# Where v's first copies and the tail groups' turns are issued in the opening of a segment-recurrent attention kernel

## The chip, the cores and the metric

The kernel runs on one core of one Trainium2 chip. The metric is the device time of one execution in microseconds; lower is better. Several executions of each kernel are timed, and their median counts.

## The reference, cut to what matters

A pre-norm block: attention over segments of 32 tokens, in which 8 memory rows are carried from each segment to the next, and then a dense part with a squared ReLU. x is 2048 x 640 in bf16, 32 heads of 128; Wq, Wk and Wv are 640 x 4096, Wo is 4096 x 640.

```python
for s in range(n_seg):                       # 64 segments, in order
    xs = x[:, s*32:(s+1)*32]                 # layernormed
    h = concatenate([mem, xs], axis=1)       # 8 memory rows + 32 tokens
    q, k, v = h @ Wq, h @ Wk, h @ Wv         # per head
    p = softmax(where(mask, q @ k.T * Dh**-0.5, -1e9))
    o = (p @ v) @ Wo
    mem = o[:, :8]                           # the next segment needs this
    outs.append(o[:, 8:])
h = x + concatenate(outs)
h2 = h + (relu(layernorm(h) @ w1 + b1) ** 2) @ w2 + b2
```

## The kernel before

**Rows.** A segment's 40 rows are split. Its 8 memory rows and its first 24 tokens make the 32 main rows, which must wait for the segment before. Its last 8 tokens, the tail, depend on no memory. Four segments make a block; the tails of a block's four segments are 32 rows, and those of four blocks, 128 rows, are a tail group: ("t", 0) to ("t", 3). For a tail group, `load_tail_rows` loads the rows, `ln_stats` takes the statistics (two on VectorE, their aggregation there, and two small steps on GpSimd for the inverse root, L174 and L175), `ln_norm` writes the normalized rows `xn` on VectorE (L188), and `ln_transpose` turns them on TensorE (`pt`, L118) and lets ScalarE copy the result to `hTt` (L218). There is one buffer for `xn`.

**Order.** Each engine executes its instructions in the order in which the program writes them; no scheduler moves them. Waits between engines and the DMA queues go over semaphores. SyncE issues nearly all loads and stores, and one that must wait holds back all issued behind it.

**The opening.** `start()` (L788) computes the first segment's q, k and v and, beside that, the q, k or v rows of tails. It has three streams, each over the five chunks of 128 rows of one weight as they arrive: `stream("v")`, `stream("q")`, `stream("k")`. For a chunk, a stream multiplies the main rows (two banks `pa`, n = 0 and 1) and block 0's tail rows (two more banks of `pa`), and then runs up to `k` closures from the list `units`. The four banks of `pa` are one PSUM buffer, so a stream cannot begin before the one ahead of it has been copied out. After the last chunk of v, VectorE copies the two main banks to `v` (L814) and ScalarE the two tail banks to `row` tiles (L263 by way of `tail_out`), with a DMA to the scratch tensor `vt_d` behind each (L360, on ScalarE's queue for block 0). After q and k, ScalarE copies all four banks, VectorE transposes each copy into `qT` or `kT` (`flip`), and GpSimd moves the tail parts.

`units` holds matmuls that fill TensorE while the weights arrive: `tail_units(b, "v")` are ten closures of four matmuls, two accumulations of five, for block b's tails; each accumulation ends in `tail_out`, a copy by ScalarE. Those v tails of later blocks are kept in places that are free in the beginning (`parked`: five slices of `hnT0`, then `ht0`, `oTts` and others), and are stored to `vt_d` later. `row` tiles come from `rowtile()`, four buffers in turn, and a tile is free again when its transpose or its store is done. `ps` tiles come from `mm` (three banks), `pc` from the bank that later holds `sm` and `pw`.

On SyncE's queue, in the order of issue: x rows, Wv, the second tail group's rows, Wq, the third group's rows (`load_tail_rows(2)`), Wk, Wo in eight pieces (`load_wo`), the next block's x rows, then block 0's tails of v read back from `vt_d` in part (`tails_v_in`; the first part on ScalarE's queue, L414), and the fourth group's rows from within step 0.

**Steps.** `step(b, sp)` then takes one segment: projections of q, k, v where `start` has not done it, scores, softmax (`soft1`, `soft2`), values, the 16 output rounds over Wo (`wo_rounds`, accumulating in `pw`), the token rows' softmax (`tokens_sum`), and `mem_to_hT`, in which VectorE and ScalarE turn the 8 new memory rows into the next step's input (L294 to L297). `run(fill, n)` puts further tail matmuls between these; `late`, `mid`, `owed`, `soon` and `stores` are other lists of closures that a step runs at fixed places. For step 0, the one with `ready`, three places of `run(fill, n)` take 2, 3 and 3 closures, and the rest follows behind output round 12.

Of the kernel before, what the change touches and what calls it, by code (L numbers as in the profile page):

```python
# [16 lines left out]
def kernel(  # L17
# [238 lines left out]
    def rowtile():  # L256
        return s2.tile([128, 512], BF16, tag="row", name="row", bufs=4)
# [38 lines left out]
        for a in range(2):  # L296
            nc.vector.tensor_tensor(out=hT4[64 * a:64 * a + 64, :, sp, 0:M], in0=tr[0:64, a, :, 0:M], in1=tc_[:, a], op=ALU.add)  # L297

    fill, late, mid, owed = [], [], [], [[], [], []]

    def run(q, n):
        while n > 0 and q:
# [21 lines left out]
    def tail_quarters(b, which, n, u):  # L324
        if which == "v":
            wr = wv[:].rearrange("p (c k n u f) -> p c n k u f", c=DC, k=G, n=2, u=2)
            cols = lambda c, k: wr[:, c, n, k, u]
        else:
            w = {"q": wq, "k": wk}[which]
            wr = w[:].rearrange("p (c g j n k e) -> p c n k g j e", c=DC, g=G, n=2, j=4, k=4)  # L330
            cols = lambda c, k: wr[:, c, n, k, 2 * u:2 * u + 2]
        st = {}

        def unit(cs):
            def f():
                if 0 in cs:
                    st["ps"] = mmtile()
                for c in cs:
                    for k in range(4):
                        matmul(st["ps"][32 * k:32 * k + 32, 0:256], lhsT=tail_rows(b, c), rhs=cols(c, k),  # L340
                               start=(c == 0), stop=(c == DC - 1))
                if DC - 1 in cs:
                    row = rowtile()
                    evac_row(which, row[:, 0:256], st["ps"][:, 0:256])
                    if which == "v":
                        nc.sync.dma_start(out=vt_d[b, 2 * n + u], in_=row[:, 0:256])
                        return
                    dst = tails[b][which]
                    late.append(lambda: nc.vector.transpose(out=dst[:, n * 16 + u * 8:n * 16 + u * 8 + 8, 0:32],
                                                            in_=row[:, 0:256].rearrange("p (h e) -> p h e", e=32)))  # L350
            return f
        return [unit(cs) for cs in ((0, 1), (2, 3), (4,))]

    def tail_out(b, which, n, ps):
        kept = which == "v" and 0 < b and len(parked) > 0
        row = parked.pop(0)() if kept else rowtile()[:]
        evac_row(which, row, ps)
        if which == "v":
            def store(eng=nc.sync):
                eng.dma_start(out=vt_d[b, 2 * n:2 * n + 2].rearrange("j r f -> r j f"),  # L360
                              in_=row.rearrange("r (j f) -> r j f", j=2))
            if kept:
                stores.append(store)
            else:
                store(nc.sync if b else nc.scalar)
            return
        if n == 0:
            tails.setdefault(b, {})[which] = s2.tile([128, H, 32], BF16, tag=which + "Tt", name=which + "Tt")
        dst = tails[b][which]
        late.append(lambda: flip(row, dst, n))  # L370
# [86 lines left out]
    def step(b, sp, v=None):  # L457
# [123 lines left out]
        token_scores(0)  # L581
        if ready:
            load_tail_rows(3)
            run(fill, 2)
        if not ready:
            proj(wv, "half", lhs, 0, ps0, 2, DC)
            nc.scalar.copy(out=v[:, 0:512], in_=ps0[:])
# [8 lines left out]
        if not last:  # L596
            soft1(1)
        if ready:
            run(fill, 3)
        po = pop.tile([128, G, 512], F32, tag="po", name="po")  # L600
        if not ready:
            proj(wv, "half", lhs, 1, ps1, 2, 3)
# [33 lines left out]
        wo_rounds(main, pw, 6, 8)  # L636
        if ready:
            tokens_sum()
        run(fill, 3 if ready else 1)
        wo_rounds(main, pw, 8, 12)  # L640
        if ready:
            run(fill, len(fill) - 6)
# [145 lines left out]
    def start():  # L788
# [11 lines left out]
        def stream(which, w, dst, k=0):  # L800
            pa = pop.tile([128, 4, 512], F32, tag="po", name="pa")
            for c in range(DC):
# [6 lines left out]
                if c < DC - 1:  # L809
                    run(units, k)  # L810
                    run(late, 100)
            for n in range(2):
                if which == "v":
                    nc.vector.tensor_copy(out=v[:, n * 512:(n + 1) * 512], in_=pa[:, n, :])  # L814
                else:
                    row = rowtile()[:]
                    evac_row(which, row, pa[:, n, :])
# [5 lines left out]
                for n in range(2):  # L823
                    tail_out(0, which, n, pa[:, 2 + n, :])

        ln_stats(("t", 1))
        ln_norm(("t", 1))
        ahead = [tail_units(1, "v"), tail_units(2, "v", (mmtile, lambda: chn.tile([128, 512], F32, tag="ch", name="pc")))]
        units += [a[n * DC + c] for c in range(DC) for a in ahead for n in range(2)]
        stream("v", wv, None, 4)  # L830
        units += tail_units(3, "v")
        units.append(lambda: ln_transpose(("t", 1))())
        units += tail_units(4, "v") + tail_units(5, "v") + tail_units(6, "v")
        run(units, 10)
        load_tail_rows(2)
        load_w(wk, A_Wk)
        load_wo()
        load_x(1)
        stream("q", wq, qT, 7)
        ln_stats(("t", 2))  # L840
        ln_norm(("t", 2))
        for n in range(2):
            spread(n)
        units += tail_units(7, "v")
        units.insert(9, lambda: ln_transpose(("t", 2))())
        units += tail_units(1, "q") + tail_units(8, "v")
        run(units, 14)
        tails_v_in(0, nc.scalar, 0, 1)
        tails_v_in(0, nc.sync, 1, 4)
        stream("k", wk, kT, DC)  # L850
        units += tail_units(1, "k")
        run(units, 100)
        return v
# [19 lines left out]
    for b in range(NB):  # L873
        for sp in range(4):
# [3 lines left out]
            if b == 0:  # L878
# [12 lines left out]
                    mid.append(lambda: ln_norm(1))  # L891
                if sp == 3:
                    ln_turn(1)
            elif b < NB - 1:
                if sp == 0:
                    fill += tail_units(b + 1, "q")[0:DC] + tail_quarters(b + 1, "q", 1, 0)
# [148 lines left out]
```

## Time and profile before

| | us |
|---|---|
| median of three timed runs | 955.13 (953.6 to 955.96) |
| the profiled execution, its own time | 958.96 |
| span of its trace | 957.2 |
| TensorE busy in the span | 929.5 (97%) |
| VectorE busy | 702.1 (73%) |
| ScalarE busy | 546.6 (57%) |
| GpSimd busy | 257.3 (27%) |

Times count from the start of the span. In the profile PE is TensorE's matmuls, PEld its weight loads, DVE VectorE, ACT ScalarE, POOL GpSimd, SP SyncE; "SPq" and "ACTq" in a view of DMAs or of a timeline are the instructions with which these engines issue DMAs. A row of a timeline has the start, the time from the first to the last instruction of the group, engine, line, operation, the tile written and the tiles read, the count, and in brackets how long the engine idled before it and what ended that. L114 and L118 are the lines of the helpers for matmul and transpose, so matmuls are told apart by their tiles: `ps<-wv,hTt` is a v tail unit, `pa<-wq,hT` the stream of q, `pw<-wo,oT` an output round. PEclk is the clock that was granted to TensorE, 1.00 for full speed.

### The profile page before, as it was taken

The page shows a single profiled execution, that of the slowest core. Times are in us where ns is not written, and L with a number is a line of the kernel's source. Part 1 is how long each engine was busy: PE and PEld are TensorE (multiplying, and loading weights), DVE is VectorE, ACT ScalarE, POOL GpSimd, SP SyncE. Part 2 cuts the span into 40 slices and gives each one's busy share as a digit, 9 for nine tenths or more (in the row PEclk, how much of TensorE's full clock was granted, in tenths as well). Part 3 has the DMA queues.
Part 4 walks back from the last instruction along what each step waited for, and adds up shares of the span by engine and source line. Part 5 has one row for each costly group of instructions (what it writes and reads, how often), then busy time and mean ns, then how long its engine had stood idle before and what let it go on. Part 6 is the DMA issues. An engine that isn't in the chain of part 4 may idle for free.

```text
span 957.2 us, 57556 instructions
## 1 busy us (share of the span) xinstructions
PE 929.5 (97%) x25883; PEld 569.8 (60%) x25883; DVE 702.1 (73%) x2136; ACT 546.6 (57%) x1342; POOL 257.3 (27%) x798
## 2 busy tenths in 40 slices
PE   5799999999999999999999999999999998999998
PEld 2346566666566666665666666666666565555555
DVE  3157788888888888888888787878788888476532
ACT  2446666666666666666666666666666665523321
POOL 1012222222222222222222222222222233254300
PEclk9899999999999999999999999999999999999999
DMA  9963210101010101010101010101010110643320
GB/s 357 404 201 96 61 34 9 34 9 34 9 33 10 34 9 34 10 34 9 31 11 32 11 32 10 32 12 31 11 32 11 53 43 21 201 111 85 94 55 28
DMA packets 60710, 56.74 MB, mean 59 GB/s; under 512 B 27560, under 2 KB 56624, under 8 KB 58544
## 3 DMA queue, kind: packets, MB, share of 16 engines
q1 hardware_dynamic: 59776, 52.74, 18.4%
q8 instruction: 202, 3.31, 1.5%
q14 instruction: 44, 0.36, 0.1%
q10 hardware_dynamic: 688, 0.33, 0.1%
HBM read 38.37 MB, written 9.44 MB: 50 GB/s over the span
## 4 chain that ended last, share of the span: by engine, by line
PE 92%; DVE 3%; DMA 2%; ACT 1%; issue 1%; POOL 0%; ACTq 0%; DVEq 0%
PE ps L114 62%; PE pw L114 16%; PE y L114 6%; PE po L114 5%; DMA xt<-in_A_x_dram 2%; PE sm L114 1%; PE pa L114 1%; DVE lnst L170 0%; DVE wk L968 0%; DMA vt_d<-row 0%; ACT otc L295 0%; DVE kTt L266 0%; DVE qT L266 0%; DVE otr L294 0%; DVE kT L266 0%
## 5 line engine op out<-in xcount | busy, mean ns | idle before, releaser
L114 PEld LDWEIGHTS <-hT 128*32 128x32 bf16 x8358 | 219.4, 96 | 136.5 <-DVE hT L297 10.4
L114 PE MATMUL pw<-wo,oT 128*32 128x320 bf16 x4224 | 178.7, 301 | 0.2
L114 PE MATMUL ps<-wv,hT 128*32 128x512 bf16 x2520 | 177.8, 380 | 0.2 <-ACT row L483 0.2
L114 PE MATMUL ps<-wq,hT 128*32 128x512 bf16 (+1 forms) x3143 | 160.9, 337 | 4.6 <-DVE hT L297 4.5
L114 PE MATMUL ps<-wk,hT 128*32 128x512 bf16 (+1 forms) x2575 | 160.3, 374 | 0.0
L652 POOL TENSOR_TENSOR pkt<-ek,rk 128x64 bf16<-128x64 bf16 x64 | 19.2, 300 | 411.4 <-DVE rk L650 398.2
L114 PEld LDWEIGHTS <-oT 128*32 128x32 bf16 x4224 | 97.0, 96 | 54.2 <-DVE oT L252 19.5
L266 DVE STREAM_TRANSPOSE qT<-row 128x512 bf16<-128x512 bf16 x128 | 89.9, 703 | 27.7 <-ACT row L261 24.6
L261 ACT ACTIVATE row<-ps 128x512 bf16<-128x512 f32 (+1 forms) x170 | 94.1, 562 | 17.7 <-PE ps L114 11.9
L967 ACT ACTIVATE wv<-ps,b1f 128x512 bf16<-128x512 f32 (+1 forms) x56 | 37.5, 673 | 67.2 <-PE ps L114 66.3
L440 ACT CAST oT<-po 128x512 bf16<-128x512 f32 x128 | 74.6, 586 | 0.1
L114 PEld LDWEIGHTS <-hTt 128*32 128x32 bf16 x1660 | 45.0, 99 | 34.6 <-issue 5.7
L295 ACT COPY otc<-otr 64x40 f32<-64x40 f32 x126 | 28.0, 223 | 65.5 <-DVE otr L294 65.0
L451 POOL COPY qz<-qT 128x96 bf16<-128x96 bf16 x126 | 33.3, 265 | 115.0 <-DVE mx L502 57.8
L114 PEld LDWEIGHTS <-v 32*128 32x128 bf16 x4064 | 42.1, 91 | 33.0 <-issue 18.4
L263 ACT CAST row<-ps 128x512 bf16<-128x512 f32 (+1 forms) x113 | 61.1, 557 | 1.1 <-PE ps L114 0.4
L114 PE MATMUL y<-wq,wk 128*128 128x320 bf16 x448 | 61.1, 299 | 0.0
L626 DVE TENSOR_REDUCE zk<-ek 128x8 f32<-128x320 bf16 x64 | 31.1, 486 | 38.3 <-ACT ek L625 38.3
L483 ACT CAST row<-ps 128x256 bf16<-128x256 f32 x126 | 40.8, 375 | 31.4 <-PE ps L114 30.4
L608 ACT CAST v<-ps 128x512 bf16<-128x512 f32 x63 | 36.9, 586 | 29.8 <-PE ps L114 29.8
L266 DVE STREAM_TRANSPOSE kT<-row 128x512 bf16<-128x512 bf16 x65 | 45.7, 703 | 10.8 <-ACT row L263 7.5
L114 PEld LDWEIGHTS <-wk 128*128 128x128 bf16 x448 | 40.6, 98 | 19.9 <-issue 5.0
(112 smaller groups left out, 1625.2 us busy)
## 6 DMA issues: line engine op xcount, KB each, us to landing
wv<-in_A_Wv_dram SPq DMA_DIRECT2D x5, 1024.0 KB
wq<-in_A_Wq_dram SPq DMA_DIRECT2D x5, 1024.0 KB
wk<-in_A_Wk_dram SPq DMA_DIRECT2D x5, 1024.0 KB
vt<-vt_d SPq DMA_DIRECT2D x60, 64.0 KB
xt<-in_A_x_dram SPq DMA_DIRECT2D x18, 160.0 KB
wo<-in_A_Wo_dram SPq DMA_DIRECT2D x2, 1280.0 KB
wq<-in_B_w_dram SPq DMA_DIRECT2D x1, 2080.0 KB
o_all<-o SPq DMA_DIRECT2D x128, 15.0 KB
```

The source lines that it names most:

```text
L114: nc.tensor.matmul(*a, **k)
L261: nc.scalar.mul(out=row, in_=ps, mul=scale)
L263: nc.scalar.copy(out=row, in_=ps)
L266: nc.vector.transpose(out=dst[:, n * 16:(n + 1) * 16, 0:32], in_=row.rearrange("p (h e) -> p h e", e=32))
L295: nc.scalar.copy(out=tc_[:, a], in_=tr[64:128, a, :, 0:M])
L440: nc.scalar.copy(out=oTg[:, n, :, :, M:NK], in_=po[:, :, n * 128:(n + 1) * 128].rearrange("p g (j q) -> p g j q", q=32))
L451: nc.gpsimd.tensor_copy(out=d.rearrange("p a (j f) -> p a j f", j=3)[:, :, :, 0:M], in_=src[:, :, 0:3, :])
L483: nc.scalar.copy(out=row[:, u * 256:(u + 1) * 256], in_=ps[:, u * 256:(u + 1) * 256])
L608: nc.scalar.copy(out=v[:, 512:1024], in_=ps1[:])
L626: nc.vector.tensor_reduce(out=zk[:], in_=ek[:], op=ALU.add, axis=AX.X)
L652: nc.gpsimd.tensor_tensor(out=pkt[:], in0=ek[:, :, SEG:NK], in1=rk[:].unsqueeze(2).to_broadcast([128, HG, TL]), op=ALU.mult)
L967: nc.scalar.activation(out=r[:, 0:w], in_=ps[:, 0:w], func=ACT.Relu, bias=b1f[:, fc:fc + 1], scale=1.0)
```

## The change

- After the stream of v, ScalarE and no longer VectorE copies the two main banks; so ScalarE copies all four.
- `tail_out` lets VectorE copy the two v tail banks of block 2.
- The second tail group, ("t", 1): statistics and norm are written behind the stream of v, and no longer ahead of it; its turn comes behind eight of block 3's ten v tail units, and no longer behind all ten, and two empty closures stand a little behind it in the list; six closures and not ten are run ahead of the loads of Wk.
- The third tail group, ("t", 2): statistics and norm are written inside the stream of q, behind its second chunk's units, and no longer behind that stream; its turn is put at the end of the units that are left from the stream of q, ahead of block 7's, and no longer behind block 7's ninth.
- Fifteen closures and not fourteen are run between the streams of q and k; within the stream of k six per chunk and not five.
- In step 0 the three places take 4, 2 and 2 closures of `fill`, not 2, 3 and 3.
- From step 3 of block 0 on, two slices of `hnT0` serve as row tiles (`spare`), one each, for the next two tail banks or quarters that would take a buffer from `rowtile()`.

```diff
-    fill, late, mid, owed = [], [], [], [[], [], []]
+    fill, late, mid, owed, spare = [], [], [], [[], [], []], []
...
                 if DC - 1 in cs:
-                    row = rowtile()
+                    row = spare.pop(0) if spare else rowtile()
                     evac_row(which, row[:, 0:256], st["ps"][:, 0:256])
...
     def tail_out(b, which, n, ps):
         kept = which == "v" and 0 < b and len(parked) > 0
-        row = parked.pop(0)() if kept else rowtile()[:]
-        evac_row(which, row, ps)
+        row = parked.pop(0)() if kept else spare.pop(0) if spare else rowtile()[:]
+        if which == "v" and b == 2:
+            nc.vector.tensor_copy(out=row, in_=ps)
+        else:
+            evac_row(which, row, ps)
...
         if ready:
             load_tail_rows(3)
-            run(fill, 2)
+            run(fill, 4)
...
         if ready:
-            run(fill, 3)
+            run(fill, 2)
...
-        run(fill, 3 if ready else 1)
+        run(fill, 2 if ready else 1)
...
                     run(units, k)
                     run(late, 100)
+                if which == "q" and c == 1:
+                    ln_stats(("t", 2))
+                    ln_norm(("t", 2))
             for n in range(2):
                 if which == "v":
-                    nc.vector.tensor_copy(out=v[:, n * 512:(n + 1) * 512], in_=pa[:, n, :])
+                    nc.scalar.copy(out=v[:, n * 512:(n + 1) * 512], in_=pa[:, n, :])
...
-        ln_stats(("t", 1))
-        ln_norm(("t", 1))
         ahead = [tail_units(1, "v"), tail_units(2, "v", (mmtile, lambda: chn.tile([128, 512], F32, tag="ch", name="pc")))]
         units += [a[n * DC + c] for c in range(DC) for a in ahead for n in range(2)]
         stream("v", wv, None, 4)
+        ln_stats(("t", 1))
+        ln_norm(("t", 1))
         units += tail_units(3, "v")
-        units.append(lambda: ln_transpose(("t", 1))())
-        units += tail_units(4, "v") + tail_units(5, "v") + tail_units(6, "v")
-        run(units, 10)
+        units.insert(8, lambda: ln_transpose(("t", 1))())
+        units.insert(11, lambda: None)
+        units.insert(12, lambda: None)
+        for b in (4, 5, 6):
+            units += tail_units(b, "v")
+        run(units, 6)
         load_tail_rows(2)
...
         stream("q", wq, qT, 7)
-        ln_stats(("t", 2))
-        ln_norm(("t", 2))
         for n in range(2):
             spread(n)
-        units += tail_units(7, "v")
-        units.insert(9, lambda: ln_transpose(("t", 2))())
-        units += tail_units(1, "q") + tail_units(8, "v")
-        run(units, 14)
+        units.append(lambda: ln_transpose(("t", 2))())
+        units += tail_units(7, "v") + tail_units(1, "q") + tail_units(8, "v")
+        run(units, 15)
         tails_v_in(0, nc.scalar, 0, 1)
         tails_v_in(0, nc.sync, 1, 4)
-        stream("k", wk, kT, DC)
+        stream("k", wk, kT, 6)
...
                 if sp == 3:
                     ln_turn(1)
+                    spare += [hnT0[:, c, :] for c in range(2)]
```

From step 1 on, the instructions stand in the same order on every engine as before.

## The prediction

> **What bounds the kernel now.** I read the page first: it says that TensorE is busy nearly throughout, and its slices say where it isn't.
>
> ```profile
> span 957.2 us, 57556 instructions
> PE 929.5 (97%) x25883; PEld 569.8 (60%) x25883; DVE 702.1 (73%) x2136; ACT 546.6 (57%) x1342; POOL 257.3 (27%) x798
> PE   5799999999999999999999999999999998999998
> PEclk9899999999999999999999999999999999999999
> DMA  9963210101010101010101010101010110643320
> ```
>
> A slice is 24 us. Only the first two show a PE below 9, a granted clock below full, and DMA engines at 9. All that the change moves lies there and in step 3 of block 0. I therefore read the timeline of PE next, over the first 110 us, with what ended each idle stretch:
>
> ```profile
> 20.41 2.34 PE L114 MATMUL ps<-wv,hTt 128*32 128x512 bf16 x40
> 24.93 0.87 PE L114 MATMUL pa<-wq,hT 128*32 128x512 bf16 x8 [2.17 <-ACT row L263]
> ...
> 28.11 2.75 PE L114 MATMUL ps<-wv,hTt 128*32 128x512 bf16 x24 [0.81 <-ACT hTt L218]
> ...
> 45.16 0.45 PE L118 MATMUL pt<-ident,xn 128*128 128x128 bf16 x5 [3.75 <-DVE xn L188]
> ...
> 56.73 2.33 PE L114 MATMUL ps<-wk,hTt 128*32 128x512 bf16 x40
> ...
> 62.33 1.00 PE L114 MATMUL pw<-wo,oT 128*32 128x320 bf16 x24
> ...
> 64.42 1.26 PE L114 MATMUL pw<-wo,oT 128*32 128x320 bf16 x32
> ...
> 67.70 1.26 PE L114 MATMUL ps<-wq,hT 128*32 128x512 bf16 x20 [0.73 <-DVE hT L297]
> ```
>
> Three waits are the opening's own: 2.17 us before Wq's first chunk, 0.81 us for the turned second tail group, 3.75 us for the normalized third. 24 matmuls took 2.75 us at 28.11, 40 took 2.34 us at 20.41: the clock. The windows view, cut where the clock changed, shows it:
>
> ```profile
> 21.75:25.16 3.41, 1.24 (x25) 0.54 (x21) 1.40 (x3) 1.17 (x2) 0.00 (x0) 1.00 1.02 423
> 25.16:28.58 3.42, 2.61 (x29) 0.95 (x21) 0.00 (x0) 2.32 (x4) 0.00 (x0) 0.50 1.00 407
> 28.58:31.99 3.41, 3.41 (x40) 1.19 (x36) 0.00 (x0) 0.91 (x2) 0.00 (x0) 0.50 1.05 411
> 45.64:49.06 3.42, 3.42 (x36) 1.38 (x36) 0.00 (x0) 2.16 (x3) 0.00 (x0) 0.50 1.07 363
> ```
>
> (Length, busy time of PE, PEld, DVE, ACT, POOL, granted clock, DMA share, GB/s.) A window with PE busy 1.24 of 3.41 us was followed by half clock; one of 2.61 of 3.42 us did not end it; full ones did. The waits cost twice: 6.73 us idle, then 10.25 us at half clock.
>
> **The opening's compute path.** From 20.41 to the end of Wk's tail units (56.73 + 2.33 = 59.06) PE takes 38.65 us. Off go 6.73 us of idling and half of the 9.44 us of matmuls at half clock (10.25 less the 0.81 idle inside), 4.72 us: 27.2 us of matmuls at full clock remain, the same in number after the change. Now the edits. The chain of waits shows how the first wait came about:
>
> ```profile
> 20.90 0.58 POOL lnrs L175
> ...
> 21.50 0.45 DVE xn L188
> 21.95 1.21 DVE v L814 x2
> ...
> 23.24 0.59 ACT row L263
> ...
> 23.86 0.40 ACTq L360
> ```
>
> v's copies on DVE stand behind the second group's norm, which waits for its rows; ACT's two tail banks wait for v; PE's first Wq matmul waits for ACT. After the change ACT takes all four banks, from the end of stream v's last matmul, about 0.2 us after the next ones' start at 20.41. Its four q evictions show the pace:
>
> ```profile
> 39.52 2.06 ACT L261 ACTIVATE row<-pa 128x512 bf16<-128x512 f32 x4 [0.71 <-PE pa L114]
> ```
>
> So 2.06 us plus the store's issue between the last two (0.40 and some gaps, together 0.6): pa is free at 23.3 rather than 24.9. PE has then run 24 tail matmuls instead of 40, to 21.8, and idles 1.4-1.5 us. The two tail banks given to DVE take about 0.6 us each there, before the norm; xn comes at 23.3, and PE asks for it only after Wq's first chunk and two units (24.6): hidden by 1.3 us. The turned group then has two units and the next chunk's sixteen matmuls (some 1.3 us) over ACT's first copy; the 0.81 us goes, at most 0.1 stays.
>
> The third group is now normalized in stream q, on DVE ahead of q's flips. Its rows are issued right behind Wq:
>
> ```profile
> 6.46 12.54 SPq L132 DMA_DIRECT2D wq<-in_A_Wq_dram  x5
> 19.41 0.54 SPq L150 DMA_DIRECT2D ht<-in_A_x_dram  x1
> ```
>
>  At 420 GB/s that queue (Wv, Wq and the x tiles, 11 MB from 2 us on, with a slower first 6 us) is through at about 32.5; the norm (two statistics 0.87, their sum 0.2, POOL 0.23 and 0.58, xn 0.45, with gaps 2.5 us) ends at 35.0, and q's rows reach DVE only at 34. PE reaches the turn, 27.2 us of matmuls being spread as before, at 35.4. If rows and norm came 2 us later, PE waited 2 us of the 3.75; I take 0.2. POOL's two small rsqrt steps move ahead of qT's copies with it, and nobody waits for those before the scores. Six units per chunk and the inserted empty units change only the order of matmuls: nothing. Sum of the path: 27.2 + 1.45 + 0.3 = 28.95 us, to 49.4: 9.7 us earlier than 59.06.
>
> **What is late next.** That isn't the gain, since the same queue still has to bring Wo. The windows view again, its last columns above all:
>
> ```profile
> 59.50:60.00 0.50, 0.50 (x35) 0.17 (x18) 0.50 (x2) 0.49 (x1) 0.00 (x0) 1.00 0.98 266
> 60.00:60.50 0.50, 0.17 (x4) 0.00 (x0) 0.15 (x2) 0.32 (x2) 0.29 (x1) 1.00 0.14 49
> ```
>
> The engines are full to 60.0 and nearly idle at 60.0-60.5: Wo's last piece lands at about 60.2, whatever PE does, as the bytes ahead of it are the same. Wo is 5.2 MB (32 x 128 x 640 in bf16); at some 340 GB/s (363 at 45.64, 266 at the end) it fills 44.7 to 60.2, so Wk is in before the new path uses its last chunk (46.0). The first half of Wo is there at 52.4, when the new path wants it (62.33 - 9.7 = 52.6), but the second output rounds, at 64.42 before, would come at 54.7 and need the second half piece by piece; the last six matmuls start at 60.3. Before, the accumulation ended at 65.68 and the block turn began at 66.60 behind VectorE's softmax of the tokens:
>
> ```profile
> 66.19 0.48 DVE L626 TENSOR_REDUCE zk<-ek 128x8 f32<-128x320 bf16 x1 [0.54 <-ACT ek L625]
> 66.60 0.57 DVE L294 STREAM_TRANSPOSE otr<-pw 128x160 f32<-128x160 f32 x2
> ...
> 68.60 0.87 DVE L170 BATCH_NORM_STATS2 lnst<-ht 128x6 f32<-128x320 bf16 x2
> ```
>
> After, that softmax is done by 57; the turn starts at 60.7 and step 1, 1.10 us on (66.60 to 67.70), at 61.8: **5.9 us earlier**. The fourth group's statistics (68.60, so 62.7 now) need rows that SyncE loads behind Wo:
>
> ```profile
> 60.23 3.17 SPq L148 DMA_DIRECT2D ht<-in_A_x_dram  x4
> ```
>
> Four issues of 0.8 us, the last ones freed by Wo's last landings, would end near 61.7, and the rows be there 1 to 2 us on: VectorE, with q's flips queued behind its statistics, might stand for 0 to 0.8 us. I count 0, as the next term covers it.
>
> **The clock again.** From 54.9 to 60.3 PE has 26 short output matmuls, 0.9 us. A 3.41 us stretch of that is busier than 26% nowhere in the middle, below the 1.24 of 3.41 us that halved the clock above. So it halves between 58.4 and 61.8. One window at half clock loses 1.7 us, of which the wait for the turn hides up to 1.1; a second follows if the first is partly idle. Ends: 0.6 and 2.8 us; I take 1.6.
>
> **Rows that are spare.** In step 3 of block 0 ACT waited for a row buffer whose store was under way:
>
> ```profile
> 108.97 0.65 ACT L483 CAST row<-ps 128x256 bf16<-128x256 f32 x2 [0.91 <-DMA vt_d<-row]
> 108.03 0.27 PE L114 MATMUL sm<-kT,qz 128*32 128x40 bf16 x16
> 110.98 0.26 PE L114 MATMUL po<-pTm,v 32*128 32x8 bf16 x16 [0.18 <-DVE pTm L518]
> 120.52 0.27 PE L114 MATMUL sm<-kT,qz 128*32 128x40 bf16 x16
> 122.80 0.26 PE L114 MATMUL po<-pTm,v 32*128 32x8 bf16 x16
> ```
>
> Scores to values took 2.95 us there, 2.28 us a step later. Two spare rows give 0.6 us (0 to 0.67). Moving fill units within step 0 of the block only fills PE's gaps earlier; their number is the same.
>
> **Sum.** 5.9 - 1.6 + 0.6 = 4.9 us. The profiled execution took 958.96 us (span 957.2 and 1.76 around it), so 954.1 for its like; against the median of 955.13: **950.2 us**. Own ends: gate 2.8 and no spare gain, 952.1; gate 0.6, 949.2.
>
> **The rivals.** (a) The clock stays full, if the short output bursts keep it: no single gap there would be longer than about 1.6 us (5.4 us less 0.9 of work, in three or more waits). Row 21.75:25.16, half clock after a window with 2.17 us of idling in one piece, speaks against it. Gain 5.9 - 0.5 (VectorE then does wait for the fourth group) + 0.6 = 6.0: 949.1. Chance 0.15. The Trainium skill, TensorE: Matmul & The Clock Gate, section on HAM oscillation, is on this rival's side: it gives some 3.4 us of idling as what throttles, and the trace, with 2.17 us, does not agree. (b) The timed executions of before have a shorter opening than the profiled one, which is 3.8 us above their median. If fewer half-clock windows are the reason, up to 4.7 us of the opening are gone there already, while the new end is held at 60.2 by Wo; with half of it the gain is 2.5: 952.6, with all 0.2: 954.9. Against it: the 3.75 us wait alone empties most of a window wherever that falls. No change, chance 0.22. (c) Slower: SyncE's loads share semaphores with ACT's transfers.
>
> ```profile
> SPq L163 <- DMA vt<-vt_d: 7.5, 4, 5.7
> 47.43 3.16 ACTq L414 DMA_DIRECT2D vt<-vt_d  x4
> ```
>
> In the new order Wo's third load waits for ACT's first vt load, the fifth to seventh for the other three. ACT issues them after the third group's turn, by my path at 39-42, and they land 5.7 us later, by 48; two Wo loads queued ahead last to 52.4. Past that point every microsecond delays Wo by one; break-even is 4.9 us later, at 57, and a slip to 61 gives 959. It needs ACT some 13 us late: 0.07, with whatever else holds SyncE.
>
> **How the numbers follow.** Forecast 0.56, (a) 0.15, (b) 0.22, (c) 0.07. Differences below 0.3% (2.9 us) can't be told from none here: faster needs under 952.3, which the forecast's own range meets and (b) mostly does not. Faster 0.69, same 0.23, slower 0.08. The range leaves out (c), most of (b)'s upper half and the unlikeliest end of (a): 948.3 to 953.8; forecast and (a) alone, 948.3 to 952.1.
>
> **What would show it.** Right: PE's first Wq chunk at 23.3; no wait for DVE xn near 40; Wk's tail units over at about 49; a wait of `pw` on `wo`'s DMA near 55 to 60; a half-clock window after 58; step 1 at 62-63.5; no wait on vt_d<-row near 108. Wrong: Wo landing before 58 or after 62; pa waiting for ACT after 23.8; the third group's norm still ending a PE wait; steps 1 to 3 longer than before by more than the gate.

## The result: 2.5 us faster, about half of the forecast

The changed kernel took 952.86 us (median of 22 executions) against 955.4 (22): ratio 0.9975, interval 0.9965 to 0.9984. In two later comparisons it was 950.33 against 953.3 (0.9968, 0.9953 to 0.9982) and 951.02 against 953.09 (0.9978, 0.9963 to 0.9993). So 2 to 3 us are gained, where 4.9 were forecast; the first median, 952.86, lies inside the whole range on record and 0.8 us above the end of the forecast's own one (952.1). Its profiled execution took 952.75 (span 950.9), 6.2 less than the profiled one of before. The gap between 6.2 and 2.5 is what has to be explained.

PE's timeline of the changed kernel, the opening, with the rows that answer to those of before:

```profile
19.60 1.46 PE L114 MATMUL ps<-wv,hTt 128*32 128x512 bf16 x24
22.54 0.61 PE L114 MATMUL pa<-wq,hT 128*32 128x512 bf16 x8 [1.47 <-ACT row L263]
...
23.95 0.45 PE L118 MATMUL pt<-ident,xn 128*128 128x128 bf16 x5
24.33 0.61 PE L114 MATMUL ps<-wv,hTt 128*32 128x512 bf16 x8
...
35.72 0.45 PE L118 MATMUL pt<-ident,xn 128*128 128x128 bf16 x5
36.61 1.26 PE L114 MATMUL ps<-wv,hTt 128*32 128x512 bf16 x20 [0.44 <-ACT oTt L263]
...
47.40 2.34 PE L114 MATMUL ps<-wk,hTt 128*32 128x512 bf16 x40
...
56.78 0.72 PE L114 MATMUL pw<-wo,oT 128*32 128x320 bf16 x14 [1.48 <-DMA wo<-in_A_Wo_dram]
57.68 0.31 PE L114 MATMUL pw<-wo,oT 128*32 128x320 bf16 x2 [0.18 <-DMA wo<-in_A_Wo_dram]
58.54 0.45 PE L114 MATMUL pw<-wo,oT 128*32 128x320 bf16 x6 [0.55 <-DMA wo<-in_A_Wo_dram]
59.39 0.31 PE L114 MATMUL pw<-wo,oT 128*32 128x320 bf16 x2 [0.40 <-DMA wo<-in_A_Wo_dram]
60.33 0.53 PE L114 MATMUL pw<-wo,oT 128*32 128x320 bf16 x6 [0.62 <-DMA wo<-in_A_Wo_dram]
60.48 2.94 PE L114 MATMUL ps<-wv,hTt 128*32 128x512 bf16 x24
62.95 1.89 PE L114 MATMUL ps<-wq,hT 128*32 128x512 bf16 x20
```

The 2.17 us wait is 1.47, those of 0.81 and 3.75 are gone. Wk's tail units are over at 49.74 (59.06 before), and then PE waits five times for Wo; the last piece is in at 60.3, as before. Behind it 24 fill matmuls take 2.94 us: half clock. The windows view shows how little PE did before that (length, busy PE, PEld, DVE, ACT, POOL, granted clock, DMA share, GB/s):

```profile
19.61:23.02 3.41, 1.94 (x40) 0.88 (x36) 1.87 (x5) 2.24 (x5) 0.79 (x2) 1.00 1.02 423
53.73:57.15 3.42, 1.95 (x60) 1.10 (x55) 2.82 (x6) 0.73 (x2) 0.00 (x0) 1.00 1.07 362
57.15:60.56 3.41, 1.66 (x28) 0.54 (x23) 0.08 (x1) 0.00 (x0) 0.00 (x0) 1.00 0.77 258
60.56:63.97 3.41, 3.41 (x40) 2.76 (x35) 1.82 (x7) 1.97 (x5) 1.57 (x4) 0.50 0.22 73
```

For comparing kernels I take the turns: the end of VectorE's second L297 operation, which completes a step's input. VectorE's timeline has them; first the turns of steps 1, 2, 4 and 5 of the kernel before, then of the changed one:

```profile
67.22 0.42 DVE L297 TENSOR_TENSOR hT<-otr,otc 64x40 bf16<-64x40 f32 x2
79.01 0.43 DVE L297 TENSOR_TENSOR hT<-otr,otc 64x40 bf16<-64x40 f32 x2
...
103.16 0.42 DVE L297 TENSOR_TENSOR hT<-otr,otc 64x40 bf16<-64x40 f32 x2
115.65 0.43 DVE L297 TENSOR_TENSOR hT<-otr,otc 64x40 bf16<-64x40 f32 x2
```

```profile
61.53 0.43 DVE L297 TENSOR_TENSOR hT<-otr,otc 64x40 bf16<-64x40 f32 x2
74.83 0.42 DVE L297 TENSOR_TENSOR hT<-otr,otc 64x40 bf16<-64x40 f32 x2
...
98.69 0.42 DVE L297 TENSOR_TENSOR hT<-otr,otc 64x40 bf16<-64x40 f32 x2 [0.29 <-ACT otc L295]
110.56 0.42 DVE L297 TENSOR_TENSOR hT<-otr,otc 64x40 bf16<-64x40 f32 x2
```

The turn behind step 0 (that of step 1) is 5.69 us earlier. The next step gives 1.5 back, 13.29 us for 11.79: the half-clock window. Steps 2 and 3 bring 0.3, and from step 4 to step 5 come 0.6. At step 5 the changed kernel is 5.09 ahead (110.98 for 116.07), and it stays 4.5 to 5.8 ahead to the last turn. The three terms of the sum, 5.9, 1.6 and 0.6, are all there, between these two executions, as 5.7, 1.5 and 0.6.

### The profile page after: what moved, and what is told of

Same layout as the page of the kernel before. It is cut to its first block, busy times and chain, and to the rows that moved or that the text cites. A ratio compares the mean times of both kernels' runs of the same rounds, so it can differ in the third digit from the quotient of the medians.

```text
span 950.9 us, 57556 instructions
## 1 busy us (share of the span) xinstructions
PE 927.1 (97%) x25883; PEld 571.7 (60%) x25883; DVE 704.2 (74%) x2136; ACT 546.0 (57%) x1342; POOL 256.7 (27%) x798
## 3 DMA queue, kind: packets, MB, share of 16 engines
q8 instruction: 202, 3.31, 1.5%
## 4 chain that ended last, share of the span: by engine, by line
PE 92%; DMA 3%; DVE 2%; ACT 1%; SPq 1%; issue 1%; POOL 0%; ACTq 0%; DVEq 0%
PE ps L114 62%; PE pw L114 16%; PE y L114 6%; PE po L114 5%; DMA vt_d<-row 1%; PE sm L114 1%; DMA wo<-in_A_Wo_dram 1%; SPq L163 1%; DMA vt<-vt_d 1%; PE pa L114 1%; DVE wk L975 0%; DVE lnst L170 0%; DMA xt<-in_A_x_dram 0%; ACT otc L295 0%; DVE otr L294 0%
## 5 line engine op out<-in xcount | busy, mean ns | idle before, releaser
L263 ACT CAST row<-ps 128x512 bf16<-128x512 f32 (+1 forms) x111 | 60.2, 558 | 1.7 <-PE ps L114 0.9
```

The costliest lines, as they stand in the source:

```text
L263: nc.scalar.copy(out=row, in_=ps)
```

## The experiments

Times are medians beside executions of the kernel before in the same comparison. That kernel took 953.3 us beside its own repetition, the changed kernel again and each part by itself; 953.72 beside the half of Wo, the first two tries at the clock and the third group with spare rows; 953.51 beside its third profile, the kernel without spare rows and the two ways on; 953.09 beside the last three kernels of the section on the clock. A turn is given by its end, the second operation of its row; the expectations give those of steps 4 and 5 by the end of the first operation, 0.23 us earlier, for all kernels alike. The turn behind step 0, which some expectations call the turn of step 0, is the one called that of step 1 above.

### The kernel before again, and a third time

```diff
(no edit)
```

> The kernel before, unchanged, profiled once more: how typical was its first profile (958.96 us against a median of 955.4, three half-clock windows in the opening, the turn behind step 0 over at 67.65)? Theory 1, fewer windows in most executions: time 954 to 956.5, one or two half-clock windows instead of three, the turn over at 64.5 to 66.5, and the stretch from there to the end as long as before within 0.7 us. Theory 2, the opening is always like that and the difference lies in the later steps: the turn over at 67.4 to 67.8 and the rest 2 to 3 us shorter.

Measured: 952.95 us against 953.3. The turn behind step 0 ends at 66.22, 1.4 us before that of the first profile, and the opening has two half-clock windows:

```profile
23.07:26.48 3.41, 1.42 (x21) 0.74 (x21) 0.20 (x1) 2.21 (x4) 0.00 (x0) 1.00 1.01 420
26.48:29.89 3.41, 2.60 (x29) 0.81 (x32) 0.00 (x0) 1.82 (x4) 0.00 (x0) 0.50 1.00 405
29.89:33.31 3.42, 3.42 (x40) 1.31 (x36) 0.00 (x0) 0.39 (x1) 0.00 (x0) 0.50 1.06 404
40.13:43.55 3.42, 1.53 (x32) 0.52 (x20) 3.15 (x6) 2.68 (x6) 0.58 (x2) 1.00 0.99 410
43.55:46.96 3.41, 1.55 (x29) 0.92 (x33) 0.77 (x3) 1.06 (x2) 1.70 (x6) 1.00 1.06 369
```

The 3.75 us wait stands there unchanged (to 45.41), but a border between two windows falls into it: each has 1.5 us of work, and the clock stays. In each trace the changes of the clock lie a whole number of 3.41 us apart: 25.16, 31.99, 45.64 and 49.06 in the first profile (2, 4 and 1 times 3.41), 26.48 and 33.31 here (twice). The wait before Wq's first chunk ends at almost the same time in both (24.93 and 25.06), so where the waits fall among the windows differs from execution to execution. Theory 1 says the right thing on the opening and theory 2 on the rest: from the turn of step 5 to the last one this execution took 693.6 us and the first profile 697.0. So much differs between two executions of one kernel.

> The kernel before, unchanged, a third profile. By the theory that its first profile stood for few executions: two half-clock windows in the opening (three in about one execution of four by the granted clocks), and the turn behind step 0 over at 65.8 to 66.6; the 3.75 us wait near 41 to 45 stands in it in any case.

Measured: 953.86 us, the turn at 67.85, three windows. The expectation of two missed: three are not rare. Each timed execution lists its granted clock, and the profiled ones tell how to read it: 0.994 and 0.995 had three half-clock windows, 0.996 two, 0.998 one, 1.0 none (I count 0.997 as two and 0.999 as none). Of 97 timed executions of the kernel before in these four comparisons, 39 so had three windows, 39 two and 19 one: 2.2 in the mean. A straight line of the time over the number of windows, with a level of its own for each comparison, gives 1.82 us per window (standard error 0.15). One window more or less is about two thirds of what the change brought.

### The changed kernel again

```diff
(no edit)
```

> The changed kernel, unchanged, profiled once more. By the forecast the turn behind step 0 is over at 61.9 to 62.1 whatever the clock does, because Wo's last piece lands at 60.0 to 60.5; one or two half-clock windows follow and make the step-1 projections 0.6 to 2.8 us later. Theory 3, the loss against the forecast lies in the kernel after: the turn at 63 or later, or three windows, and 954 or more.

Measured: 950.33 us. The turn ends at 62.27; Wo's last piece holds it as forecast. Behind it stand two half-clock windows:

```profile
55.84:59.25 3.41, 1.48 (x22) 0.56 (x22) 1.36 (x3) 0.47 (x1) 0.00 (x0) 1.00 0.95 322
59.25:62.67 3.42, 2.66 (x27) 1.78 (x30) 1.17 (x5) 0.75 (x3) 0.01 (x1) 0.50 0.40 134
62.67:66.08 3.41, 3.41 (x37) 2.67 (x33) 1.58 (x4) 1.46 (x4) 2.35 (x6) 0.50 0.25 73
```

The halved window at 59.25 has 2.66 us of work and is followed by another. From this turn to the next are 14.19 us, 2.4 more than the 11.79 of the kernel before. By the granted clocks of 46 timed executions in three comparisons the changed kernel has 1.4 windows in the mean (25 with two, 15 with one, 6 with none), at 1.2 us each by the same fit (standard error 0.2).

### Each part by itself

```diff
 # the first kernel: v's copies only
-                    nc.vector.tensor_copy(out=v[:, n * 512:(n + 1) * 512], in_=pa[:, n, :])
+                    nc.scalar.copy(out=v[:, n * 512:(n + 1) * 512], in_=pa[:, n, :])
...
-        evac_row(which, row, ps)
+        if which == "v" and b == 2:
+            nc.vector.tensor_copy(out=row, in_=ps)
+        else:
+            evac_row(which, row, ps)
 # the second kernel: the third group only
+                if which == "q" and c == 1:
+                    ln_stats(("t", 2))
+                    ln_norm(("t", 2))
...
-        units += tail_units(7, "v")
-        units.insert(9, lambda: ln_transpose(("t", 2))())
+        units.append(lambda: ln_transpose(("t", 2))())
+        units += tail_units(7, "v")
```

> Only ScalarE's copies of v and VectorE's two tail banks; the norms, turns, counts and spare rows as in the kernel before. Wait before Wq's first chunk 1.4 us for 2.17 us. If the two ends overlap (the bytes of Wo hold the end at 60.3 whoever removes the first waits): the half-clock windows at 25 to 32 are gone, Wk's tail units over at 54 to 55.5, the turn at 63 to 64, some 3.5 to 4.5 us of the 5.7 from this part alone. If the windows stay: tail units over at 57.5 to 58, the turn at 66 to 66.5. If the parts are additive and small: 0.7 to 1.2 us.

> Only the third tail group's statistics, norm and turn at their new places; v's copies, the second group, counts and spare rows as in the kernel before. The 3.75 us wait near 41 to 45 and the half-clock window behind it are gone, the two windows at 25 to 32 stay. Overlapping ends: Wk's tail units over at 53 to 54.5, the turn at 62 to 63, 4.7 to 5.5 of the 5.7 us from this part alone, so that the two parts alone sum to far more than both together (8 to 10 against 5.7). Additive parts: about 3 us here and 2.7 with the other part.

Measured: v's copies alone 951.05 us (0.9971, 0.9955 to 0.9987), the third group alone 949.71 (0.9956, 0.9943 to 0.9968), in the comparison in which the whole change was at 0.9968. Wk's tail units are over at 55.10 and 53.96, the turn ends at 63.69 and 62.54. (With v's copies alone the wait before Wq's first chunk was 0.57 us, where 1.4 were expected.) The two gains are 2.3 and 3.6 us, 5.8 in sum, and that of both together is 3.0: the parts overlap. Wo ends step 0 near 62 in the whole change, and the third group alone already comes close to that. The third group alone was even 0.6 us below the whole change, which the intervals do not tell apart. PE's timeline of the third group alone:

```profile
51.61 2.35 PE L114 MATMUL ps<-wk,hTt 128*32 128x512 bf16 x40
...
57.22 1.00 PE L114 MATMUL pw<-wo,oT 128*32 128x320 bf16 x24
...
59.31 1.11 PE L114 MATMUL pw<-wo,oT 128*32 128x320 bf16 x25
60.63 0.45 PE L114 MATMUL pw<-wo,oT 128*32 128x320 bf16 x7 [0.21 <-issue]
```

TensorE comes to the output rounds 4.3 us later than in the changed kernel (57.22 for 52.88), finds Wo there, and runs step 1 at full clock, 11.80 us between the turns, although its two half-clock windows near 25 to 32 are still there.

### What holds the end of step 0

```diff
-        for h0, k in ((0, 8), (16, 8), (1, 4), (17, 4), (9, 2), (25, 2), (13, 2), (29, 2)):
+        for h0, k in ((0, 8), (16, 8)):
...
+    nc.vector.memset(wo[:, 1:32:2, :], 0.0)
     v0 = start()
```

> The changed kernel with only Wo's first two pieces loaded (the even heads); the odd heads are zeroed on VectorE in its idle time ahead of the stream of v, so the products with them are zeros. If Wo's bytes hold the end of step 0: no wait of pw for Wo near 55 to 60, the turn over at 57.8 to 58.8 (softmax of the tokens by 57.3, then the turn) instead of 62.0 to 62.3, no half-clock window behind it, and the turn of step 5 at 105 to 107 instead of 110.8 to 112.1. If Wo was only the last of several late things: the turn no earlier than 60.5.

This kernel leaves out half of Wo, so its output is not the block's; only its times are of use. Measured: 946.12 us in one execution. The turn ends at 58.47 and that of step 5 at 105.91:

```profile
58.04 0.43 DVE L297 TENSOR_TENSOR hT<-otr,otc 64x40 bf16<-64x40 f32 x2
69.83 0.42 DVE L297 TENSOR_TENSOR hT<-otr,otc 64x40 bf16<-64x40 f32 x2
...
105.49 0.42 DVE L297 TENSOR_TENSOR hT<-otr,otc 64x40 bf16<-64x40 f32 x2
```

No half-clock window, 11.79 us from turn to turn. Wo's bytes hold the end, by 3.5 us. That the clock is lost through the same wait is not shown by this execution alone, since 6 of the 46 of the changed kernel have no half-clock window either; the next section tests it.

### The clock

The first try put idle matmuls into the wait for Wo.

```diff
+        def warm(n):
+            if ready:
+                d = mmtile()
+                for i in range(n):
+                    k = i % 4
+                    matmul(d[32 * k:32 * k + 32, 0:192], lhsT=lhs(0), rhs=wv[:, 512 * k:512 * k + 192], start=(i < 4), stop=(i >= n - 4))
+        warm(56)
         wo_rounds(main, pw, 8, 12)
         if ready:
             run(fill, len(fill) - 6)
-        wo_rounds(main, pw, 12, 16)
+        warm(36)
+        wo_rounds(main, pw, 12, 14)
+        warm(36)
+        wo_rounds(main, pw, 14, 16)
```

> The changed kernel with 128 matmuls of 192 columns (some 2.6 us in all) into a PSUM tile that nobody reads, put in front of output rounds 8, 12 and 14 of step 0, that is into the waits for Wo's pieces. If the clock is lost because TensorE is too little busy there: the turn stays at 61.9 to 62.5, no half-clock window between 56 and 70, the turn of step 2 at 73.7 to 74.2 instead of 75.25 or 76.46, and the time 1.3 to 2.5 us below the changed kernel's, 3.7 to 5.5 below that of the kernel before in the same comparison. If the clock falls for another reason (the burst behind the wait, the DMAs): windows as in the changed kernel, and the same time or up to 0.5 us more.

Measured: 950.86 us, 2.9 below the kernel before, the turn at 64.39. It tells little on the clock, since PE stood still amid the added matmuls, waiting for nothing that the profile shows:

```profile
58.21 1.13 PE L114 MATMUL ps<-wv,hT 128*32 128x192 bf16 x31 [2.30 <-issue]
```

Half clock followed this stall too (58.85:60.34 has 0.50). The second try moves real work.

```diff
             load_tail_rows(3)
-            run(fill, 4)
+            run(fill, 2)
...
-            run(fill, 2)
+            run(fill, 1)
...
-        wo_rounds(main, pw, 8, 12)
-        if ready:
-            run(fill, len(fill) - 6)
-        wo_rounds(main, pw, 12, 16)
+        if ready:
+            run(fill, 2)
+        wo_rounds(main, pw, 8, 10)
+        if ready:
+            run(fill, 1)
+        wo_rounds(main, pw, 10, 12)
+        if ready:
+            run(fill, 1)
+        wo_rounds(main, pw, 12, 14)
+        if ready:
+            run(fill, 1)
+        wo_rounds(main, pw, 14, 16)
```

> The changed kernel with the 15 tail units of step 0 placed otherwise: 2, 1, 4, then 1 each in front of output rounds 10, 12 and 14, and 5 behind round 15. The same work, spread into the wait. By the clock theory the window of 3.41 us ahead of the turn holds two units more (about 0.45 us): if that is enough, no half-clock window and the turn of step 2 at 73.7 to 74.2; if not, one window, at 75 to 76, and 0 to 1 us gained from one unit fewer behind the turn. If the wait's idling doesn't matter: no difference from the changed kernel beyond 0.3 us.

Measured: 949.77 us (0.9959, 0.9945 to 0.9974); not one of nine executions has a granted clock below 1.0. The turn ends at 61.91, as in the changed kernel, and that of step 2 at 74.17. Four tail units, and not the five expected, stand behind output round 15 in the trace, where the changed kernel has six. The two stretches of 3.4 us ahead of the turn hold 2.1 us of work each:

```profile
53.70:57.10 3.40, 2.15 (x66) 1.03 (x59) 2.80 (x7) 0.97 (x3) 0.00 (x0) 1.00 1.07 365
57.10:60.50 3.40, 2.10 (x40) 1.03 (x36) 0.29 (x1) 0.83 (x2) 0.00 (x0) 1.00 0.77 261
```

Two kernels were then run beside it on one chip, the changed one and the kernel before with idle matmuls in its waits:

```diff
+        def busy(n):
+            d = mmtile()
+            for i in range(n):
+                k = i % 4
+                matmul(d[32 * k:32 * k + 32, 0:256], lhsT=main(0), rhs=wv[:, 512 * k:512 * k + 256], start=(i < 4), stop=(i >= n - 4))
...
         load_x(1)
+        busy(40)
         stream("q", wq, qT, 7)
...
-        units.insert(9, lambda: ln_transpose(("t", 2))())
+        units.insert(9, lambda: (busy(88), ln_transpose(("t", 2))()))
```

> The kernel before with 128 matmuls of 256 columns into a PSUM tile that nobody reads: 40 in front of the stream of q (some 1.1 us, into the wait of 2.17 us) and 88 in front of the third group's turn (2.4 us, into the wait of 3.75 us). Nothing else is changed, and every wait ends when it did. If the half-clock windows are what the kernel before loses beside its idling, at 1.8 us each by its timed executions and 2.2 of them in the mean: no window in the opening, Wk's tail units over at 54 to 55, the turn behind step 0 over at 62.5 to 64, and 3 to 4.5 us below the kernel before, as much as the whole change. If the windows cost little or come from something else than too little work: 0 to 1 us, or a loss of up to 2 us where the added instructions stall TensorE's fetch.

> The changed kernel beside the one with the spread fill, on the same chip. By its granted clocks so far it has 1.4 half-clock windows in the mean behind the wait for Wo, at 1.5 to 2 us each: 2.4 to 3.2 us below the kernel before, and 1.5 to 2.8 above the spread fill, unless the spread fill gives part of that back in steps 3 to 10, as its trace showed (1 us): then 0.8 to 1.8 above it.

> The changed kernel with step 0's tail units spread into the wait for Wo, once more, beside the changed kernel on the same chip: no half-clock window in nearly all executions, 3.6 to 4.6 us below the kernel before, 0.8 to 2.8 below the changed kernel. If the windows at the end of step 0 didn't matter: within 0.5 us of the changed kernel.

Measured against 953.09 us: the busied kernel before 950.1 (0.997, 0.9959 to 0.9981), the changed kernel 951.02 (0.9978, 0.9963 to 0.9993), the spread fill 948.93 (0.9958, 0.9943 to 0.9974), again without a half-clock window in all its six executions. The changed kernel gained a little less than the 2.4 to 3.2 us expected of it, and the spread fill is 2.1 us below it; 1.4 windows at 1.2 us are 1.6 of that, and two units fewer behind the turn are at most 0.4. PE's timeline of the busied kernel before:

```profile
22.16 1.26 PE L114 MATMUL ps<-wv,hT 128*32 128x256 bf16 x40
23.72 0.62 PE L114 MATMUL pa<-wq,hT 128*32 128x512 bf16 x8 [0.30 <-ACT row L263]
...
38.53 2.58 PE L114 MATMUL ps<-wv,hT 128*32 128x256 bf16 x88 [0.70 <-ACT oTt L263]
41.56 0.45 PE L118 MATMUL pt<-ident,xn 128*128 128x128 bf16 x5 [0.45 <-DVE xn L188]
...
51.45 2.33 PE L114 MATMUL ps<-wk,hTt 128*32 128x512 bf16 x40
```

PE gets no useful work done in those waits, and yet its half-clock windows are gone (nine of eleven executions at 0.999 or 1.0), Wk's tail units are over at 53.78 and the turn at 62.37. By the medians of one comparison, 3.0 us for 2.1, that is the whole gain of the change, within the intervals, without the change. The opening of this one trace was lucky: the wait for ScalarE's row ended at 23.72, and at 24.93 to 25.07 in the three profiles of the kernel before, because the second group's rows came sooner (VectorE began their statistics at 18.16 for 19.37 in the first profile), which nothing in the edit does.

### The spare rows

```diff
-                    spare += [hnT0[:, c, :] for c in range(2)]
```

> The changed kernel without the two spare rows. From the turn of step 4 to that of step 5 the kernel before took 12.41 to 12.49 us and the changed one 11.78 to 11.87, but the two kernels with one part alone, that have no spare rows either, 11.88 and 12.03. If the spare rows bring the 0.6 us: 12.4 to 12.5 here, with waits of ScalarE on vt_d<-row between 90 and 112. If the rows come free in time because everything stands earlier against their stores: 11.8 to 12.05, and waits on vt_d<-row of 0.3 us at most.

Measured: 952.81 us in one execution; 11.93 us from the turn of step 4 to that of step 5, and no wait on `vt_d<-row` there:

```profile
99.91 0.42 DVE L297 TENSOR_TENSOR hT<-otr,otc 64x40 bf16<-64x40 f32 x2
111.84 0.42 DVE L297 TENSOR_TENSOR hT<-otr,otc 64x40 bf16<-64x40 f32 x2
```

The 0.6 us come without the spare rows. The busied kernel before, which has none and an opening as early, took 11.89 there and had no such wait either, and three profiles of the changed kernel took 11.78 to 12.00; the third profile of the kernel before took 12.18, so 0.6 is itself not the same in every execution. The other try put the rows beside the third group alone:

```diff
 # on top of the third group alone
+                    spare += [hnT0[:, c, :] for c in range(2)]
...
-                    row = rowtile()
+                    row = spare.pop(0) if spare else rowtile()
...
```

> Only the third group's new places and the two spare rows; v's copies, the second group's places and all counts as in the kernel before. If the parts of the change overlap as the runs so far say, this has the whole gain without the wait that loses the clock: turn of step 0 at 62.4 to 62.7 as with the third group alone, 0.6 us more at the turn of step 5 (109.2 to 109.4), and 4 to 4.8 us below the kernel before, 1 to 1.8 below the changed kernel. If the parts add: slower than the changed kernel by 1 us or more.

Measured: 950.08 us (0.9956, 0.994 to 0.9971), the same ratio as without the rows. From step 4 to step 5 it took 11.95 us, with 12.03 for the third group alone. The turn of step 5, expected at 109.3 (109.5 by the second operation), came at 111.29: the rows brought nothing, and the step behind the turn took 12.53 us for 11.80 with the third group alone, with short stalls of PE without a releaser (0.32 us at 71.41). Wo's last piece came at 61.04, but the turn ended at 62.58 for 62.54.

### Two ways on

```diff
 # the first kernel: the spread fill, and
-    nc.sync.dma_start(out=mem0, in_=A_mem0[0])
-    load_tail_rows(0)
+    nc.scalar.dma_start(out=mem0, in_=A_mem0[0])
+    load_tail_rows(0, nc.scalar)
 # the second kernel: the spread fill with 3, 2, 2, 2 for its 2, 1, 1, 1, and
-                for h in range((3, 1, 1, 1)[sp]):
+                for h in range((4, 1, 1, 0)[sp]):
```

> The changed kernel with its step-0 fill spread into the wait for Wo, and with the loads of the memory rows and of the first tail group issued by ScalarE, so that SyncE issues Wv's first chunk 1.2 us sooner (at about 1.1 for 2.31). If the bytes ahead of Wo's last piece set the end of step 0: Wo lands 0.6 to 1.2 us sooner, the turn is over at 60.7 to 61.3, and the time is 0.5 to 1.2 us below that of the kernel with the spread fill alone, 4.3 to 5.3 below the kernel before. If the start is bound by something else (the x rows, the queue's depth): the turn at 61.8 to 62.2 and no difference.

> The changed kernel with five tail units taken out of steps 1 to 3 into step 0's wait for Wo: 2, 1, 5, then 2 each ahead of output rounds 10, 12 and 14, and 6 behind round 15. TensorE has some 4 us idle there, five units are 1.1 us. If steps 1 to 3 are bound by TensorE: the turn of step 0 at 61.9 to 62.3, no half-clock window, and the turn of step 4 0.6 to 1.1 us earlier than with the spread fill alone (98.17), at 97.1 to 97.6. If those units only cover the turns of steps 1 to 3: no gain at step 4, or up to 0.5 us lost.

Measured: 948.86 us (0.9953, 0.9938 to 0.9968) and 949.12 (0.9958, 0.9945 to 0.9972), which the intervals do not tell apart from the spread fill alone (0.9959 and 0.9958). In the first the DMA engines are less busy sooner, 0.61 of the time in 58:59 where the changed kernel has 0.88, but the turn still ends at 62.25:

```profile
58.00:59.00 1.00, 0.86 (x21) 0.36 (x13) 0.48 (x1) 0.49 (x2) 0.00 (x0) 1.00 0.61 215
```

```profile
60.34 0.32 PE L114 MATMUL pw<-wo,oT 128*32 128x320 bf16 x3 [1.48 <-issue]
```

No wait for Wo is left; a stall of 1.48 us of PE's own, of the kind that the first try at the clock had met, takes its place. So the turn came where the second alternative had it, but for another reason. (PE's first Wq chunk came at 25.12, and it reached the output rounds at 55.15 for 53.04 in the spread fill.) In the second kernel the turn of step 4 ends at 98.27, against 98.40 and 97.39 in the two profiles of the spread fill. The 0.6 to 1.1 us did not come. That those units only cover the turns of steps 1 to 3 fits this, but two profiles of one kernel differ by 1 us here, so it is not shown.

## Why the prediction was right on the mechanism and wrong on the size

**The mechanism and the place.** The places were as worked out. In the three profiles of the changed kernel PE's first Wq chunk came at 22.54 to 23.42 (23.3 forecast), the tail units ended at 49.74 to 50.37 (49.4), Wo's last piece was in at 60.33 to 60.85 (60.2 to 60.3), the turn ended at 61.96 to 62.67 (step 1 was to begin at 61.8), pw waited for Wo, and the clock fell behind that wait. That the tail units ended within 0.4 us of the forecast in the first of these was partly luck: the path took 30.14 us and not 28.95, with 0.8 more of idling (0.49 for Wq's last chunk and 0.44 for ScalarE among it) and 0.4 more of work, but began at 19.60 and not 20.41. It cost nothing, since Wo held the end. VectorE's wait for the fourth group's rows, counted as nothing, was 0.64 to 0.81 us in them; PE shows no wait for it.

**The step that failed** is the last one of the sum, "so 954.1 for its like; against the median of 955.13: 950.2". The mis-sized term is the 5.9 us: they were worked out on an execution with three half-clock windows in its opening (4.72 us of the path are theirs), and taken off a median of executions that have 2.2 of them, as counted in the later comparisons. The gain at the turn of step 5 was 5.09 us between the two profiled executions; 0.8 of a window at 1.82 us is 1.5 less, and 0.4 of a window more behind the wait, at 1.2 us, 0.5 less: 3.1, where the three comparisons gave 2.5, 3.0 and 2.1; what is left, 0.1 to 1.0 us, is not accounted for. Rival (b) had this, with half of the excess gone in the timed executions, and gave 952.6; it was held at 0.22. Its reason against, that the 3.75 us wait empties most of a window wherever that falls, is what the second profile of before refutes: split by a border, it left 1.5 us of work in each of two windows, and the clock stayed.

**The term of the clock** (1.6, from 0.6 to 2.8) measured 1.5, 2.4 and 2.2 in the three traces of the changed kernel and 2.0 without the spare rows, by their turns: 13.29, 14.19, 13.97 and 13.78 us less 11.79. Those traces have one, two, two and two windows; by the fit the mean of 1.4 windows at 1.16 us is 1.6, so the value chosen holds for the mean. The reading behind it was too low: the stretch was to be busy for 26% at most, and the two windows that were followed by half clock held 1.66 and 1.48 us, 49% and 43%, more than the 1.24 us that it was compared with.

**The term of the spare rows** had about the right size and the wrong cause: ScalarE's waits near 108 are also gone where the opening is earlier and no spare rows are there, in v's copies alone, the third group alone, the busied kernel before and the kernel without the rows.

**Rival (a)**, the clock staying full, with 949.1, is what six of 46 executions of the changed kernel did. The Trainium skill's rule in TensorE: Matmul & The Clock Gate, section on HAM oscillation, some 3.4 us of idling, does not describe these runs: in the window 57.15:60.56 of the changed kernel PE was idle for 0.62 us at most in one piece, and half clock followed. Of the full-clock windows shown, those with 1.24 to 1.48 us of work were followed by half clock, those with 1.94 and more were not; between them 1.53 and 1.55 were not, and 1.66 was. Busy time is modelled, and a finer bound can't be read from it. **Rival (c)** did not happen; Wo's loads did wait for ScalarE's vt loads (2.9 us in the view of SyncE's waits), while the DMA engines were full (a share of 1.07 in 50:53.7). **Small slips**: the page's slices 34 and 40 show PE at 8 too, and of the first two only the second shows a clock below 9; the end without the spare rows is 952.0 and not 952.1. Nothing hangs on them. A gain of 0.25%, held to be too small to tell from none, was told from none by 22 executions of each kernel.

**What the gain consists of** turned out otherwise than the forecast has it. The fits give, for an execution without any half-clock window, 949.1 for the kernel before and 948.8 for the changed one in the second comparison, 949.1 and 949.1 in the last, each to about 0.4 us. For the kernel before this is extended beyond what was seen, as no execution of it had none. So the idling that the change takes from the path (6.7 us before) brings next to nothing by itself. Without the 4.72 us of its windows the first profile of the kernel before would have its turn at 62.9 (67.64 less 4.72), just behind the 61.96 to 62.67 at which Wo lets the changed kernel end step 0. The gain is then 2.2 windows at 1.82 us less 1.4 at 1.16, that is 2.4. This rests on the fit and, independently, on the busied kernel before.

**Open**: why the steps behind the opening differ by 3.5 us between executions of one kernel, and what PE waits for in its stalls of 0.2 to 2.3 us. The profile of the changed kernel lists a DMA queue of the kind "instruction" (202 packets, 3.31 MB) beside the data's; whether the stalls are waits for it is not shown.

## What to carry to other kernels

Before a saving worked out on one profiled execution is taken off a median, look at what in that execution varies: here the granted clocks of the timed executions would have shown one to three half-clock windows for the same code. Where transfers hold the end of a stage, removing idle time ahead only moves it, and where it lands matters: spread the work that is left through the new wait, so that every stretch of it keeps TensorE busy (here 2.1 us in each 3.41 kept the clock in all 15 executions, 1.66 did not). Test parts alone when a change has several; their gains need not add (here 2.3 and 3.6 us alone, 3.0 together).

## What was not expected of the hardware

In these traces the windows of 3.41 us lie on a grid of their own, and a wait of 3.75 us (41.4 to 45.2) cost a window in the first profile and none in the second, by its place in that grid. A window at half clock with 2.6 us of work did not restore the clock (26.48:29.89). PE stalled without a visible releaser for 2.30 us amid 128 added matmuls, with the DMA engines full (1.03), and for 1.48 us in another kernel with the DMA engines at 0.44. The first stall moved the turn to 64.39, 1.7 to 2.4 us behind the changed kernel's, so added filler can cost as much as the clock that it saves.
